# DeltaNet and Fourier mixing on one core: GpSimd's products and memsets on VectorE, transposed inverses as identity products, unread products ahead of the first load, inversions begun a slot sooner

## The chip, the core and the metric

The kernel runs on one core of a Trainium2 chip. A core has five engines, each with an instruction queue of its own that is worked off in order: TensorE (PE, matrix products into PSUM; PEld is its loading of weights), VectorE (DVE), ScalarE (ACT), GpSimd (POOL) and SyncE (SP, which issues transfers). They wait for one another by semaphores. The metric is the time of one execution on the device in microseconds (us); lower is better.

## The reference

Two blocks follow each other. The first is DeltaNet attention: for each of 4 batches and 8 heads, over 768 steps, with 48 numbers per head:

```python
k_n = k / (np.linalg.norm(k, axis=-1, keepdims=True) + 1e-06)
for t in range(S):
    y[:, :, t] = np.einsum('bhd,bhde->bhe', q[:, :, t], state)
    v_old = np.einsum('bhde,bhd->bhe', state, kt)
    state = state + bt[:, :, :, None] * np.einsum('bhd,bhe->bhde', kt, vt - v_old)
```

The second takes the output as x with 4 x 768 rows of 384 numbers, mixes it with a two-dimensional Fourier transform, and applies a layer norm and an MLP (384 to 1536 to 384):

```python
u = x + np.real(np.fft.fft(np.fft.fft(x, axis=1), axis=2))
un = (u - mean(u)) / np.sqrt(var(u) + 1e-06)
out = u + np.maximum(un @ w_ch1, 0.0) @ w_ch2
```

## The kernel before

**Attention in periods and rounds.** A period is 128 steps of all eight heads of one batch: 6 periods make a batch, 24 the whole (numbered g = 0 to 23). Inside a period the recurrence is turned into matrix products: with the Gram matrix of the keys (`pre_a`, in periods 0 to 11 by `gram16`, L351), the inverse of a triangular matrix, and products with it, so that only two steps per period (`step`, L671, c = 0 and 1) pass the state S on. The triangular systems of four periods are inverted together on VectorE; these four periods are a round (rounds 0 to 5). `invert16` (L451, rounds 0 to 2) inverts blocks of 16 and leaves the merging of two blocks to products on TensorE; `invert` (L392, rounds 3 to 5) inverts blocks of 32. Each starts with a memset of M (L467, L397) and a transpose of the Gram matrices (L468, L398), then runs a loop in which a product (L510, L439) and an addition (L513, L443) alternate, and ends with transposes: L516 writes the inverse into G, L518 the transposed inverse into A (L446 and L447 in `invert`).

`pre_m16` (L591) makes period g's matrix from its round's inverse. Z is the inverse with zeros in the other half of each pair (two ScalarE copies, L601). px, a product of the masked Gram matrix GU with Z, is copied as ND (L610); MT is the transposed inverse spread like Z (L614 on VectorE for period 0, otherwise L617 on ScalarE). Three groups of products with ND, MT and Z follow, and the values V are scaled by nT (L622). `pre_m` (L551) does less for periods 12 to 23: a masked copy MT (L559) and the scaled values (L562).

**The second block.** `folds` (L772) adds and subtracts halves of x for the Fourier step (L786, L788), `fourier` does its products, `mlp` (L889) the layer norm and the two matrix products, cut into pieces.

**The weights** arrive as 64-bit numbers and are converted on chip, in `weights` (L221): 12 pieces of w1 and 12 of w2, each by ScalarE copies (L272, L277), five VectorE operations (L278, L282, L283, L292, L294) and one product (L287).

**The order** of TensorE, VectorE, ScalarE and GpSimd is written out by hand, in program order; nothing reorders it. From L1082 on: keys 0 to 3, inversion 0, loads, keys 4 to 7, five products that nobody reads (`spin`, L1116), then batch 0's periods, with inversion 1 and the conversion of the weights in between (`fill`, `convert`). From batch 1 on, `period` (L991) runs six slots per period. In each slot come pieces of the two steps and of the next period's preparation, some operations of the running inversion (`advance(inv, ...)`), and pieces of the second block for the batch before, as many as `want` says. In periods that are the first or second of a round (li = 0 or 1) the keys of the next round are prepared; the inversion of the next round begins in slot 1 of li = 1.

PSUM tiles come from three tags with two buffers each: "pair" (two banks), "one" and "post". A tile that takes a buffer waits until the tile two before it under the same tag has been read. In `pre_m16` px is a "one" tile, while the products for S, for V's update, for the outputs and for turned keys with K are "pair" tiles.

Of the kernel before, what the change touches and what calls it, by code (L numbers as in the profile page):

```python
# [17 lines left out]
C = 64  # L18
L = 128
W = 32  # L20
RL = 4
# [43 lines left out]
def kernel(  # L65
# [37 lines left out]
    def ps_one():  # L103
        return ps.tile([128, 512], F32, tag="one", bufs=2, name="one")
# [87 lines left out]

    early = w2.rearrange("p c m -> p (c m)").rearrange("p (n h d) -> p n h d", h=8, d=64)
    nc.vector.memset(early[:, :, :, D:64], 0.0)
    early = [early[:, i] for i in range(9)]
# [25 lines left out]
    def weights():  # L221
# [13 lines left out]
        for last, pieces in enumerate(sets):  # L235
# [33 lines left out]
            for i in range(len(pieces) + 1):  # L269
# [10 lines left out]
                if i > 0:  # L280

                    nc.vector.tensor_scalar(num0, num0, 255, 2.0 ** 23, op0=ALU.min, op1=ALU.mult)  # L282
                    nc.vector.scalar_tensor_tensor(num0, hi0, -2 ** 31, num0, op0=ALU.bitwise_and,  # L283
                                                   op1=ALU.bitwise_or)
                    dst = pieces[i - 1][1]
                    c = dst.shape[1]
                    nc.gpsimd.tensor_tensor(dst, man0.rearrange("p (c f) -> p c f", c=c),  # L287
                                            num0.bitcast(F32).rearrange("p (c f) -> p c f", c=c),
                                            op=ALU.mult)
                    stage(i - 1 + deep)  # L290
# [60 lines left out]
    def gram16(g, KT, G):  # L351
# [5 lines left out]
        if first:  # L357
            GU = GXs["O"][:, g]
        else:
            GU = wk.tile([128, 8, C], F32, tag="GX", bufs=4, name="GU")  # L360
            nc.gpsimd.memset(GU[:, :, 0:V16], 0.0)
        GXs[g, 16] = GU
# [10 lines left out]
        for hh in range(2):  # L373
# [3 lines left out]
            else:  # L377
                nc.scalar.activation(dst[rw], src[rw, :, :, W:C], ACT.Copy)
        if g == 2 * RL - 1:
            yield  # L380
# [11 lines left out]
    def invert(r):  # L392
# [3 lines left out]
        M = wk.tile([128, W, W], F32, tag="M", name="M")  # L396
        nc.gpsimd.memset(M, 0.0)  # L397
        nc.vector.transpose(A, G.rearrange("p m s -> p s m"))  # L398
# [52 lines left out]
    def invert16(r):  # L451
# [14 lines left out]
        A, M, Ad, Md = whole(A2), whole(M2), blocks(A2), blocks(M2)  # L466
        nc.gpsimd.memset(M2, 0.0)  # L467
        nc.vector.transpose(A, G.rearrange("p m s -> p s m"))  # L468
# [47 lines left out]
        nc.vector.transpose(G.rearrange("p m s -> p s m"), M.rearrange("p t s -> p s t"))  # L516
        yield
        nc.vector.transpose(A.rearrange("p m t -> p t m"), M)  # L518
        rounds[r] = (A, G, nT)
        yield  # L520
# [30 lines left out]
    def pre_m(g):  # L551
# [9 lines left out]
                                op=ALU.mult)  # L561
        nc.gpsimd.tensor_tensor(V.rearrange("p c j d -> p (c j) d"),  # L562
                                V.rearrange("p c j d -> p (c j) d"),
# [27 lines left out]
    def pre_m16(g):  # L591
# [3 lines left out]
        K, GU = Ks[g % 3], GXs.pop((g, 16))  # L595
        MTd, Md, nT = rounds[r]
        m8 = slice(8 * li, 8 * li + 8)
        tags = ("QT", "LQ") if g < 2 * RL else ("WT", "WT")
        Z = wk.tile([128, 8, 2, W], F32, tag=tags[0], bufs=2, name="Z")
        for e in range(2):  # L600
            nc.scalar.activation(Z[:, :, e, :], Md[:, m8, :], ACT.Copy, scale=m_blk[:, e:e + 1])  # L601
        if g != 2 * RL:
            yield
        px = ps_one()
        for m in range(8):
            for hh in range(2):
                mm(px[full[hh], C * m:C * m + C], GU[full[hh], m, :],
                   Z[full[hh], m].rearrange("p b t -> p (b t)"), m == 0)
        ND2 = wk.tile([128, 8, C], F32, tag=tags[1], bufs=2, name="ND")
        nc.scalar.activation(ND2.rearrange("p m t -> p (m t)"), px, ACT.Copy)  # L610
        MT = wk.tile([128, 8, 2, W], F32, tag="MT", bufs=2, name="MT")
        for e in range(2):
            if g == 0:
                nc.vector.tensor_scalar(MT[:, :, e, :], MTd[:, m8, :], m_blk[:, e:e + 1], None,  # L614
                                        op0=ALU.mult)
            else:
                nc.scalar.activation(MT[:, :, e, :], MTd[:, m8, :], ACT.Copy,  # L617
                                     scale=m_blk[:, e:e + 1])

        def scaled_v():  # L620
            V = Vs.pop(g)
            (nc.vector if g < 2 * RL else nc.gpsimd).tensor_tensor(  # L622
                V.rearrange("p c j d -> p (c j) d"), V.rearrange("p c j d -> p (c j) d"),
                nT[:, m8, None].broadcast_to([128, 8, D]), op=ALU.mult)
            return V
# [146 lines left out]
    def folds(b):  # L772
# [11 lines left out]
        for t in range(TH):  # L784
            eng = nc.gpsimd if b and t < TH - 1 else nc.vector
            eng.tensor_tensor(E[:, 0, t], x[:, t], x[:, TH + t], op=ALU.add)  # L786
            yield
            eng.tensor_tensor(E[:, 1, t], x[:, t], x[:, TH + t], op=ALU.subtract)  # L788
            yield
# [198 lines left out]
    done = 0  # L988
    pm = inv = late = None

    def period(g, side):  # L991


        nonlocal pm, inv, late, done, fold
        b, n = divmod(g, NL)
# [33 lines left out]
        if not last_round and r > 1:  # L1029
            if li == 0:  # L1030
                load_beta(r + 1)
            keys = {0: ((0, 1), (2, 3), (4, 5)), 1: ((0, 1),)}.get(li, ())
            for i, (s0, s1) in enumerate(keys):
                k4 = pre_a(RL * (r + 1) + 3 * li + i)
                behind[s0].append(k4)
                pieces[s1].append(k4)
        for i in range(SLOTS):
# [5 lines left out]
            if i == 5 and n + 1 == NL:  # L1043
                o = outputs(g)
                drain(o)
                late = None
            if li == 1 and i == 1 and r > 1 and not last_round:
                inv = invert(r + 1)
# [11 lines left out]
            if b > 1:  # L1060
                want = 2 + (PIECES - KEEP - 2) * at // (SLOTS * NL)
            else:

                want = 2 + KF + (2 + 2 * KF) * at // (2 * SLOTS)
                if n > 1:
                    want = 4 + 3 * KF + (PIECES - KEEP - 4 - 3 * KF) * (at - 2 * SLOTS) // (
                        SLOTS * (NL - 2))
            for p in behind[i]:
# [7 lines left out]
    with tc.manual_schedule(engines=engines):  # L1076
# [4 lines left out]
        qs = [pre_q(g, QT6[:, g], LQ6[:, g]) for g in range(NL)]  # L1081
        ms = [pre_m16(g) for g in range(2 * RL)]  # L1082
        for g in range(RL):
            advance(keys[g])
            if g > 0:
                drain(keys[g - 1])
        drain(keys[RL - 1])
        advance(inv0, 2)
        for g in range(3):
# [21 lines left out]
        advance(keys[-1])  # L1111
        idle = wk.tile([128, DM], F32, tag="un", bufs=2, name="idle")
        nc.gpsimd.memset(idle, 0.0)
        unread = ps_post([128, 512], "unread")

        def spin(n):  # L1116

            for _ in range(n):
                nc.tensor.matmul(unread[:, 0:DM], lhsT=ident, rhs=idle, start=True, stop=True,  # L1119
                                 skip_group_check=True)  # L1120

        spin(5)

        advance(ms[0], 2)
        advance(qs[1])
# [10 lines left out]
        advance(inv1, 5)  # L1136
        drain(keys[-1])
        first = part(conv, 2 * KF + 2)
# [194 lines left out]
```

## Time and profile before

| | us |
|---|---|
| three runs, median (lowest, highest) | 760.11 (759.6, 760.41) |
| the profiled execution | 760.74 |
| its span, first to last instruction | 759.0 |
| busy in the span: ScalarE | 246.7 |
| busy in the span: GpSimd | 99.2 |
| GpSimd: 24 weight products L287 | 28.0 |
| GpSimd: 16 products of V (L562, L622) | 13.8 |
| GpSimd: 12 masked copies L559 | 12.8 |
| GpSimd: 12 folds (L786, L788) | 12.2 |
| GpSimd: memsets of M (L467, L397) | 6.0 |
| VectorE: 3 transposes L518 | 5.7 |

The profile is of one execution. Its view of groups gives, for each line, engine and shape of operand, the count, the sum and the mean time of one instruction, and what the engine waited for just before. The view by windows gives the busy time of each engine in a stretch of the span. The chain of waits is followed back from the last instruction: at each step to the instruction that released the one under view, or to the one before it on the same engine. Time on that chain is time that the span can lose; time elsewhere isn't, until the chain moves. Waits are the engine's idle time put down to the instruction that released it. For TensorE the largest of them:

```profile
PE pair L110 <- DVE S L732: 9.1, 6, 3.6
PE pair L110 <- DVE pair L745: 6.7, 3, 3.3
PE one L110 <- ACT Z L601: 6.3, 6, 2.5
PE pair L110 <- ACT QT L314: 5.6, 2, 4.6
```

The columns are the us in total, the number of waits and the longest one.

### The profile page before, as it was taken

What the parts mean: (1) busy time and instruction counts of PE and PEld (TensorE: products, weight loads), DVE (VectorE), ACT (ScalarE), POOL (GpSimd) and SP (SyncE); (2) the same over time, 40 slices, a digit from 0 to 9 for tenths busy, and PEclk for the clock granted to TensorE, in tenths of its full rate; (3) what the DMA queues carried; (4) which work ended last, traced back from release to release, by engine and by line L of the source; (5) the groups of instructions that cost most, each with busy time, mean ns of one, the idle gap of its engine ahead of it and who ended that gap; (6) DMA issues with size and microseconds to landing.
All of it is one profiled execution on the core that took longest, in us unless ns stands there. A gap on an engine that the chain in (4) does not pass through costs nothing.

```text
span 759.0 us, 23046 instructions
## 1 busy us (share of the span) xinstructions
PE 691.9 (91%) x10162; PEld 534.2 (70%) x10162; DVE 392.1 (52%) x961; ACT 246.7 (33%) x610; POOL 99.2 (13%) x138
## 2 busy tenths in 40 slices
PE   5877779697899986999999999999999999999998
PEld 4666668586667655877867768877667678777684
DVE  4966896879942499343298228178512240600000
ACT  3533662566424311223422333233223221211120
POOL 7000120322300012001110220020100110100000
PEclk9999987798999999999999999999999999999999
DMA  9832353025212312002212221011120000000000
GB/s 151 215 67 43 78 136 92 24 58 133 74 32 55 67 34 44 12 11 48 54 41 49 44 44 29 1 31 24 43 44 12 13 12 0 22 1 21 11 11 22
DMA packets 111863, 36.10 MB, mean 48 GB/s; under 512 B 101873, under 2 KB 109842, under 8 KB 111762
## 3 DMA queue, kind: packets, MB, share of 16 engines
q1 hardware_dynamic: 109938, 33.86, 20.3%
q8 instruction: 80, 1.31, 0.7%
q0 software_dynamic: 640, 0.43, 0.4%
q10 hardware_dynamic: 1184, 0.33, 0.3%
q14 instruction: 21, 0.17, 0.1%
HBM read 29.88 MB, written 4.72 MB: 46 GB/s over the span
## 4 chain that ended last, share of the span: by engine, by line
PE 74%; DVE 19%; ACT 3%; issue 3%; DMA 1%; DVEq 0%; ACTq 0%
PE po L110 24%; PE ph L110 21%; PE one L110 14%; PE pair L110 9%; PE one L113 2%; DVE M L443 2%; DVE tmp L439 2%; PE ptr L113 1%; DVE wtmp L294 1%; DVE wtmp L283 1%; PE unread L1119 1%; DMA C<-in_k_dram 1%; DVE M L513 1%; DVE wtmp L292 1%; PE pf L110 1%
## 5 line engine op out<-in xcount | busy, mean ns | idle before, releaser
L110 PE MATMUL ph<-unT,w 128*128 128x256 f32 x864 | 207.8, 392 | 0.7 <-ACT unT L911 0.7
L110 PE MATMUL po<-w,hT 128*128 128x384 f32 x576 | 204.7, 495 | 0.0
L110 PEld LDWEIGHTS ph<-unT,w 128*128 128x128 f32 x864 | 162.7, 194 | 25.5 <-issue 1.0
L110 PEld LDWEIGHTS po<-w,hT 128*128 128x128 f32 x576 | 103.5, 190 | 56.4
L921 ACT ACTIVATE hT<-ph 128x256 f32<-128x256 f32 x144 | 54.9, 382 | 148.5 <-PE ph L110 148.4
L932 DVE TENSOR_TENSOR x<-x,po 128x384 f32<-128x384 f32 x24 | 13.2, 550 | 107.0 <-PE po L110 107.0
L732 DVE TENSOR_TENSOR S<-S,pair 128x192 f32<-128x192 f32 x40 | 13.9, 348 | 73.4 <-PE pair L110 73.4
L110 PEld LDWEIGHTS one<-V,MT 64*64 64x64 f32 x768 | 29.5, 138 | 19.7 <-issue 8.9
L873 DVE TENSOR_TENSOR x<-x,one 128x193 f32<-128x193 f32 x24 | 8.5, 353 | 64.8 <-ACT Q L864 64.8
L110 PE MATMUL one<-V,MT 64*64 64x48 f32 x768 | 34.8, 225 | 3.8 <-DVE V L691 1.8
L443 DVE TENSOR_TENSOR M<-M,tmp 128x31 f32<-128x31 f32 (+15 forms) x93 | 35.1, 378 | 3.2
L439 DVE TENSOR_TENSOR tmp<-A,M 128x31 f32<-128x31 f32 (+15 forms) x93 | 33.5, 360 | 2.4
L110 PE MATMUL one<-MT,ND 64*64 64x64 f32 x768 | 29.1, 226 | 1.8 <-ACT MT L640 0.7
L691 DVE TENSOR_TENSOR V<-V,pair 128x192 f32<-128x192 f32 x33 | 11.5, 349 | 36.9 <-PE pair L110 33.2
L559 POOL TENSOR_TENSOR MT<-A,pack 128x512 f32<-128x512 f32 x12 | 12.8, 1065 | 131.1 <-PE one L110 64.4
L110 PEld LDWEIGHTS one<-dtab,F 97*128 97x128 f32 (+1 forms) x192 | 25.7, 193 | 5.3 <-ACT F L868 0.5
L110 PEld LDWEIGHTS one<-MT,ND 64*64 64x64 f32 x768 | 26.5, 141 | 2.9 <-issue 1.1
L314 ACT ACTIVATE QT<-one 128x512 f32<-128x512 f32 x24 | 14.3, 596 | 42.1 <-PE one L113 42.1
L287 POOL TENSOR_TENSOR w<-wtmp 128x384 f32<-128x384 f32 x12 | 14.6, 1217 | 89.7 <-DVE wtmp L283 89.7
L110 PE MATMUL pair<-KT 48*32 48x64 f32 (+1 forms) x1152 | 22.7, 247 | 4.0 <-ACT KT L314 3.9
L110 PEld LDWEIGHTS pair<-U,K 64*64 64x64 f32 x704 | 15.5, 135 | 15.3 <-issue 12.4
L110 PE MATMUL one<-dtab,F 97*128 97x97 f32 (+1 forms) x192 | 26.2, 277 | 0.0
(173 smaller groups left out, 1009.5 us busy)
## 6 DMA issues: line engine op xcount, KB each, us to landing
w<-in_moe_w_ch_dram SPq DMA_DIRECT2D x12, 384.0 KB
E<-in_moe_w_ch_dram SPq DMA_DIRECT2D x12, 384.0 KB
out_dram<-x SPq DMA_DIRECT2D x24, 192.0 KB
K<-in_k_dram SPq DMA_DIRECT2D x92, 48.0 KB
V<-in_v_dram SPq DMA_DIRECT2D x92, 48.0 KB
C<-in_k_dram SPq DMA_DIRECT2D x18, 192.0 KB
Q<-in_q_dram SPq DMA_DIRECT2D x18, 192.0 KB
w<-in_q_dram SPq DMA_DIRECT2D x6, 192.0 KB
```

The lines of the kernel that those rows point to most:

```text
L110: nc.tensor.matmul(o, lhsT=lhsT, rhs=rhs, start=start, stop=stop, skip_group_check=True)
L113: nc.tensor.matmul(o, lhsT=src, rhs=ident[0:src.shape[0], 0:src.shape[0]], is_transpose=True, start=start, stop=True, skip_group_check=True)
L287: nc.gpsimd.tensor_tensor(dst, man0.rearrange("p (c f) -> p c f", c=c), num0.bitcast(F32).rearrange("p (c f) -> p c f", c=c), op=ALU.mult)
L314: nc.scalar.activation(dst.rearrange("p h j t -> p (h j t)"), pt, ACT.Copy)
L439: nc.vector.tensor_tensor(t, A[:, j + 1:W, j:j + 1].broadcast_to([128, n, j + 1]), M[:, j:j + 1, 0:j + 1].broadcast_to([128, n, j + 1]), o ...
L443: nc.vector.tensor_tensor(M[:, j + 1:W, 0:j + 1], M[:, j + 1:W, 0:j + 1], t, op=ALU.add)
L559: nc.gpsimd.tensor_tensor(MT, MTd[:, m8, None, :].broadcast_to([128, 8, 2, W]), m_blk[:, None, :, None].broadcast_to([128, 8, 2, W]), op=A ...
L691: nc.vector.tensor_tensor(R4, R4, pw[:, :, 0:2 * D].rearrange("p a (j e) -> p a j e", e=D), op=ALU.subtract)
L732: nc.vector.tensor_tensor(s1v, s0.rearrange("p h j e -> p h (j e)"), pk, op=ALU.add)
L873: nc.vector.tensor_tensor(near, near, pb[:, 0, 0:MH + 1], op=ALU.add)
L921: nc.scalar.activation(hT[:, fc, :], ph, ACT.Relu)
L932: nc.vector.tensor_tensor(x[:, T, :], x[:, T, :], po, op=ALU.add)
```

## The change

- A tile `idle` of zeros is made first of all on VectorE, and four unread products run on TensorE ahead of the first transposes of keys; before the px of period 0 there are two instead of five, with `idle` as both operands instead of the identity matrix as weights.
- On VectorE instead of GpSimd: the 24 products that finish a weight piece, the memset of `idle`, the memset of GU in 8 periods, the memset of M in all rounds but the first, the product of V and nT in periods 8 to 23, and the folds of batches 1 to 3.
- Rounds 0 to 2: the transpose that made the transposed inverse (L518) is gone. `pre_m16` makes MT from products of Z with the identity matrix, 16 more products of 64x64 per period in 12 periods, in the second bank of px, which becomes a "pair" tile. MT is one copy instead of two. In period 0 the second half of Z and the copy of MT are on VectorE.
- At the start, the inversion's first transpose (L468) comes ahead of the masks of GU of keys 2 and 3, which come ahead of the inversion's further steps.
- In `period`, the last key of a round is prepared in slot 5 of li = 0 and slot 0 of li = 1 instead of slots 0 and 1 of li = 1, and the inversion begins in slot 0 of li = 1. Pieces of the second block in batch 1's six periods: up to 14, and then 13, 11, 4, 7, 7 and 6, instead of 14, then 13, 13 and four equal parts of 5.5; 62 in both cases.

```diff
@@ -191 @@
+    idle = wk.tile([128, DM], F32, tag="un", bufs=2, name="idle")
+    nc.vector.memset(idle, 0.0)
     nc.vector.memset(early[:, :, :, D:64], 0.0)
...
@@ -284 @@ weights
-                    nc.gpsimd.tensor_tensor(dst, man0.rearrange("p (c f) -> p c f", c=c),
+                    nc.vector.tensor_tensor(dst, man0.rearrange("p (c f) -> p c f", c=c),
...
@@ -358 @@ gram16
-            nc.gpsimd.memset(GU[:, :, 0:V16], 0.0)
+            nc.vector.memset(GU[:, :, 0:V16], 0.0)
...
-        if g == 2 * RL - 1:
+        if first or g == 2 * RL - 1:
             yield
...
@@ -394 @@ invert
-        nc.gpsimd.memset(M, 0.0)
+        nc.vector.memset(M, 0.0)
...
@@ -464 @@ invert16
-        nc.gpsimd.memset(M2, 0.0)
+        (nc.vector if r else nc.gpsimd).memset(M2, 0.0)
...
-        yield
-        nc.vector.transpose(A.rearrange("p m t -> p t m"), M)
-        rounds[r] = (A, G, nT)
+        rounds[r] = (None, G, nT)
...
@@ -559 @@ pre_m
-        nc.gpsimd.tensor_tensor(V.rearrange("p c j d -> p (c j) d"),
+        nc.vector.tensor_tensor(V.rearrange("p c j d -> p (c j) d"),
...
@@ -593 @@ pre_m16
         for e in range(2):
-            nc.scalar.activation(Z[:, :, e, :], Md[:, m8, :], ACT.Copy, scale=m_blk[:, e:e + 1])
+            if g == 0 and e:
+                nc.vector.tensor_scalar(Z[:, :, e, :], Md[:, m8, :], m_blk[:, e:e + 1], None,
+                                        op0=ALU.mult)
+            else:
+                nc.scalar.activation(Z[:, :, e, :], Md[:, m8, :], ACT.Copy,
+                                     scale=m_blk[:, e:e + 1])
         if g != 2 * RL:
             yield
-        px = ps_one()
+
+        px = ps_pair()
         for m in range(8):
             for hh in range(2):
-                mm(px[full[hh], C * m:C * m + C], GU[full[hh], m, :],
+                mm(px[full[hh], 0, C * m:C * m + C], GU[full[hh], m, :],
                    Z[full[hh], m].rearrange("p b t -> p (b t)"), m == 0)
+        for m in range(8):
+            for hh in range(2):
+                mm(px[full[hh], 1, C * m:C * m + C], Z[full[hh], m].rearrange("p b t -> p (b t)"),
+                   ident[full[hh], full[hh]], m == 0)
...
-        for e in range(2):
-            if g == 0:
-                nc.vector.tensor_scalar(MT[:, :, e, :], MTd[:, m8, :], m_blk[:, e:e + 1], None,
-                                        op0=ALU.mult)
-            else:
-                nc.scalar.activation(MT[:, :, e, :], MTd[:, m8, :], ACT.Copy,
-                                     scale=m_blk[:, e:e + 1])
+        if g == 0:
+            nc.vector.tensor_copy(MT.rearrange("p m b t -> p (m b t)"), px[:, 1])
+        else:
+            nc.scalar.activation(MT.rearrange("p m b t -> p (m b t)"), px[:, 1], ACT.Copy)
...
-            (nc.vector if g < 2 * RL else nc.gpsimd).tensor_tensor(
+            nc.vector.tensor_tensor(
...
@@ -782 @@ folds
-            eng = nc.gpsimd if b and t < TH - 1 else nc.vector
-            eng.tensor_tensor(E[:, 0, t], x[:, t], x[:, TH + t], op=ALU.add)
+            nc.vector.tensor_tensor(E[:, 0, t], x[:, t], x[:, TH + t], op=ALU.add)
...
@@ -1029 @@ period
-            keys = {0: ((0, 1), (2, 3), (4, 5)), 1: ((0, 1),)}.get(li, ())
...
+            if li == 0:
+                for i in range(3):
+                    k4 = pre_a(RL * (r + 1) + i)
+                    behind[2 * i].append(k4)
+                    pieces[2 * i + 1].append(k4)
+                last_key = pre_a(RL * (r + 1) + 3)
+                behind[5].append(last_key)
+            elif li == 1:
+                pieces[0].append(last_key)
...
-            if li == 1 and i == 1 and r > 1 and not last_round:
+            if li == 1 and i == 0 and r > 1 and not last_round:
                 inv = invert(r + 1)
...
-                want = 2 + KF + (2 + 2 * KF) * at // (2 * SLOTS)
-                if n > 1:
-                    want = 4 + 3 * KF + (PIECES - KEEP - 4 - 3 * KF) * (at - 2 * SLOTS) // (
-                        SLOTS * (NL - 2))
+                want = 2 + KF
+                for of in (13, 11, 4, 7, 7, 6):
+                    want += of * min(max(at, 0), SLOTS) // SLOTS
+                    at -= SLOTS
...
@@ -1080 @@
+        spin(4)
         for g in range(RL):
             advance(keys[g])
             if g > 0:
-                drain(keys[g - 1])
+                advance(keys[g - 1])
+            if g > 1:
+                drain(keys[g - 2])
+        advance(keys[RL - 1])
+        advance(inv0)
+        drain(keys[RL - 2])
         drain(keys[RL - 1])
-        advance(inv0, 2)
+        advance(inv0)
...
@@ -1109 @@
-        spin(5)
-
-        advance(ms[0], 2)
+        spin(2)
+
+        advance(ms[0])
+        drain(keys[-1])
+        advance(ms[0])
```

## The prediction

> **What bounds the kernel now.** I read the engine totals and the 40 slices first, then sums of busy time by stage, then the chain of waits inside each stage where TensorE was short of work, then the groups of VectorE and GpSimd by form, because a fixed price hides in none of the first three.
>
> From the page:
> ```profile
> PE 691.9 (91%) x10162; PEld 534.2 (70%) x10162; DVE 392.1 (52%) x961; ACT 246.7 (33%) x610; POOL 99.2 (13%) x138
> ...
> PE   5877779697899986999999999999999999999998
> ...
> DVE  4966896879942499343298228178512240600000
> ```
> TensorE is the bound from slice 16 on (303 us) and GpSimd is nearly idle. The sums by stage, cut at the places where the chain changes its nature (columns: length, then busy us of PE, PEld, DVE, ACT, POOL, then granted clock, DMA share, GB/s):
> ```profile
> 0.00:37.00 37.00, 26.59 (x370) 19.59 (x370) 25.75 (x63) 16.38 (x40) 16.11 (x42) 1.00 1.05 186
> 37.00:79.00 42.00, 30.40 (x1049) 28.24 (x1049) 28.20 (x73) 17.98 (x40) 0.00 (x0) 0.96 0.28 53
> 79.00:118.00 39.00, 28.74 (x1036) 26.02 (x1028) 34.22 (x73) 22.38 (x49) 9.09 (x8) 0.90 0.43 109
> 162.00:213.00 51.00, 42.71 (x507) 34.00 (x506) 49.12 (x124) 25.10 (x62) 14.31 (x16) 0.90 0.34 89
> 256.00:303.00 47.00, 36.87 (x737) 26.55 (x737) 43.63 (x105) 9.90 (x25) 6.91 (x7) 1.00 0.18 39
> 303.00:759.00 456.00, 446.96 (x5140) 335.62 (x5136) 167.78 (x430) 119.17 (x310) 38.96 (x50) 1.00 0.11 25
> ```
> VectorE is full in 162-213 and 256-303. TensorE idles 58 us before 303 and 9 us after. So whatever a part does after 303 is worth little unless it is TensorE work, and before 303 a part is worth what the chain there says. Three pieces of the chain of waits (start, length, what):
> ```profile
> 29.54 6.04 PE unread L1119 x10
> 35.58 1.10 PE one L110 x32
> ...
> 256.41 0.28 ACT G L346
> 256.69 0.02 issue
> 256.72 1.96 DVE A L398
> ...
> 300.73 1.85 DVE G L447
> 302.58 0.21 DVE S L732
> ```
> The first: five unread products keep TensorE until 35.58, though the Z that px needs was written by 34.31 (timeline). The second: the inversion of round 3 starts when the last key's G is copied (256.72) and holds VectorE to 302.58. Last the forms of three rows:
> ```profile
> L294 DVE TENSOR_SCALAR wtmp<-w 128x384 int32<-128x384 int32 x12 | 11.1, 926 | 0.4
> ...
> L622 DVE TENSOR_TENSOR V<-V,nT 128x384 f32<-128x384 f32 x8 | 4.4, 546 | 0.0
> ```
> ```profile
> L287 POOL TENSOR_TENSOR w<-wtmp 128x384 f32<-128x384 f32 x12 | 14.6, 1217 | 89.7 <-DVE wtmp L283 89.7
> ```
> The same product costs GpSimd 1.22 us and VectorE about 0.55. And the VectorE conversion L294, which runs beside it, takes 926 ns where the same operation on the other tile takes 473 as a mean and 347 in its undisturbed instances. Summed over all VectorE instructions that overlap a GpSimd one, the excess over undisturbed ones of the same form is about 25 us.
>
> **What the Trainium skill says.** "SBUF — State Buffer", section "Who interferes with whom": VectorE and GpSimd share one port pair as an exclusive lock, contended by VectorE operations with two SBUF inputs or in a 2-port mode. The 926 against 347 ns agrees. "GPSIMD Engine Reference", 4.1: two-input elementwise work is about twice as slow on GpSimd; 1217 against 546 ns agrees. "TensorE: Matmul & The Clock Gate", Part 1: the array runs at half clock until about 3.4 us of sustained activity, and drops back after an idle window. The trace agrees: 128x128 transposes start every 225 ns before 34.8 us, every 128 ns later, and an unread record takes 0.61 us against 0.34 for one of the same width later. The page's digit 9 in the first slices has no clock record behind it. Further clock records at half speed lie at 41.6-45.0, 109.9-123.5, 137.2-147.4, 174.7-181.5, 195.2-198.6 and 304.4-307.8 us.
>
> **The change part by part.** The profiled execution (span 759.0, 760.74 with what lies around it) is what the sum is made against; the median, 760.11, is 0.63 below it.
>
> *VectorE.* It gains 24 w products, 8 GU memsets, 5 of the M memsets, one idle memset, 16 V products and 12 folds; at 0.5, 0.08-0.2, 1.0, 1.0, 0.55 and 0.55 us that is about 12 + 1.2 + 5 + 1 + 8.7 + 6.6 = 34.5 us. It loses three transposes L518 (5.7) and most of the 25 us of stretching; the mask product L559 (1.07 us, 12 times) and rstd stay on GpSimd and keep perhaps 4 of it. Net +4 to +8 us of VectorE time, of which only what falls in full stretches counts.
>
> *TensorE.* Twelve groups of 16 identity products (64x64): a group like them takes 1.10-1.16 us in the chain, 0.95 when nothing hinders it, 1.8 at half clock; 11-14 us in all, eight groups before 160 us, four in 213-303. The copy of MT follows the second group instead of the first, but is one copy of 0.60 us instead of two of 0.50. px moves from the two "one" buffers to the two "pair" buffers that the S, K and LQ products of the loop use as well, so a px waits for the reader of the pair two before it, and the next state product waits for both ND and MT copies; queued behind it are all of TensorE's next groups. The trace of before doesn't show that wait: between 0 (TensorE idle there anyway) and 1.2 us (the copies ND and MT in sequence) per turn; I take 0.4.
>
> *0-37 us.* Four unread products ahead of load 0, cold at 1.22 us each, run from about 1.5 to 6.4 us (they wait for a memset of 1.0) and hold the first transposes from 4.81 to 6.4, those of load 1 from 6.62 to 7.5. If the clock is up by then, the six groups of 1.05 us between 6.62 and 13.03 halve, limited by the loads that land every 1.3 us, and the transpose L468 starts at about 13.1 instead of 16.65. Two masks (2 x 0.69) and three GU memsets (0.6) then stand between it and the inversion's next step on VectorE, with its square root on ScalarE (ends 18.75 now) hidden under them: that step from 18.78 to about 17. L516 ends 1.9 earlier; Z's halves are made on two engines at once (0.5 instead of 0.9); two unread products instead of five no longer outlast Z; px and the identity group take 2.2, the MT copy 0.7: first product at about 35.2 against 37.35, -2.2. If the clock is not up, 0.9 is lost at the start and the end is about +0.8. I take -1.5.
>
> *37-79.* Four turns, each +1.0 for the identity group where TensorE is on the chain, +0.15 for the copies, +0.4 for the buffers, less what falls into the stage's 11.6 us of idle (28%): about 4 x 0.75 = +3; L518 leaves the chain at 75.48 (0.94): together +2 (0 to +5).
>
> *79-118.* VectorE's chain: seven L294 lose 0.69 of stretch, seven products cost 0.5, a memset 0.2: -1.1; four turns of identity and buffer waits at +0.5: together +0.9 (-1 to +4).
>
> *118-162.* TensorE runs half-clocked for much of it. Nothing here ties the clock to the change for certain: 0, from -5 (the clock holds) to +2. Conversions: stretch gone about as much as products added, 0.
>
> *162-213.* VectorE is the bound (49.1 of 51): +6.0 for 12 products, +1.0 memset, +0.6 GU memsets, +0.5 V, against 8.3 us of stretch here: -0.2 (-3 to +3).
>
> *213-303.* The last key and the inversion start one slot sooner, and the early slots give fewer MLP pieces: priced by rows, TensorE's work between px of period 8 (213.36) and the last key's gram falls from 37.8 to 34.0, its two identity groups included; scaled to the traced 43.0, -4.3 us. The moved step takes along one load of 192 KB on SP's queue (DMA share 0.18-0.30 here, free) and on VectorE the memset M (1.0, VectorE is idle before 256). The inversion keeps its length: stretch gone 3.2, V products +1.1, folds +2.2. TensorE has 10.1 us idle in 256-303; 4.3 earlier with two further identity groups of 1.1 leaves 3-4, so TensorE allows it: -4. The 3.56 us wait at 302.83 shrinks with it, and the half clock of 304.4-307.8 with that, -1.5. Together -5.5 (-8 to -1).
>
> *303 to the end.* Bound by TensorE with 9 us idle. Inversions a slot sooner save at most the gaps at 522.75 (1.50) and 538.65 (0.82). V products now stand in VectorE's order ahead of the S updates and wait for their loads, which land 0.6 to 2.2 us after the S updates now start; the products reading S have 1.0 to 3.1 us to spare, so at most +0.5. -0.8 (-2 to +2).
>
> Sum: -1.5 + 2 + 0.9 + 0 - 0.2 - 5.5 - 0.8 = -5.1: 755.6 against the profiled 760.74, 755.0 against the median.
>
> **The rivals.** *TensorE and its pair buffers become the bound before 160 us* (the slower end): each of the eight early turns pays the whole identity group and the wait for both copies. For it: 70% TensorE share there is an average over short alternations, each of which is on the chain. Against it: the idle of 28%. At +1.8 per turn the stages to 118 give +0.8, +6 and +6 instead of -1.5, +2, +0.9; with the rest as above +6.3, 766.4 profiled, 765.8. It decides from about 1.3 us per turn, where the gain of 213-303 is used up.
>
> *The clock holds*: the added early TensorE work keeps the activity up, and the half clock at 41.6 and 109.9-123.5 goes: -2.2, +1, +0.5, -5, and the rest: about -12.5, 747.6. For it: each half-clock record follows a stretch of waits. Against: the waits of 79-118 are VectorE's and stay.
>
> *The inversion's head start is given back*: it starts 4.3 us sooner, but folds and V products lengthen it or another engine holds the S behind it; -1 instead of -5.5: 759.5. For it: 43.6 us of VectorE in 47. That the change doesn't do what it says is excluded by the instruction lists, except that the clock may not be up at load 0, which is in the bounds.
>
> **How the numbers follow.** The forecast has 0.45, with its own range 751 to 759; the slower rival 0.29; the clock 0.13; the given-back start 0.13. A difference under 0.2% (1.5 us) can't be told from none. Faster: 0.45 x 0.97 + 0.13 + 0.13 x 0.3 = 0.61; same: 0.08; slower: 0.31. The range takes in half of the rivals on either side: 747 to 766.
>
> **What would show it.** Right: the first product of period 0 at 35 us and L468 at 13; L294 near 350 ns in both forms; the round-3 transpose L398 at or before 253 with no wait over 1 us at its end; clock records near 1.0 from 7 us. Wrong: TensorE waits of about 1 us on ND or MT copies in every turn before 118 us; the conversions' stage longer than 51 us; L398 starting no sooner than about 4 us ahead of where it would, counted from px of period 8.

## The result

The changed kernel takes 770.11 us (median of 4 runs, 768.71 to 771.2) against 760.25 for the kernel before beside it: 1.013 times, 95% interval 1.0112 to 1.0149. It is slower by 9.9 us where 5.1 us less were forecast, and above the range. The profiled execution of it took 769.61 us, with a span of 767.8.

From the page of the changed kernel:

```profile
PE 700.4 (91%) x10548; PEld 543.7 (71%) x10548; DVE 395.7 (52%) x1024; ACT 243.4 (32%) x598; POOL 39.1 (5%) x72
...
PE   6677786798799898999999999999999999999998
...
PEclk8599998899899999999999999999999999999999
```

GpSimd lost 60 us of work and VectorE gained 3.6, just under the 4 to 8 of the sum; TensorE gained 8.5, where 11 to 14 were counted. What is new stands in the first slices: TensorE is less busy there and its clock lower.

The sums by stage, cut where the same places of the program lie now (columns as before):

```profile
0.00:41.00 41.00, 27.99 (x404) 20.52 (x404) 23.27 (x66) 17.20 (x43) 14.13 (x36) 0.71 1.02 176
41.00:83.00 42.00, 30.29 (x1064) 28.05 (x1064) 27.14 (x72) 13.37 (x28) 0.00 (x0) 1.00 0.24 43
83.00:123.00 40.00, 30.57 (x1100) 28.42 (x1100) 31.02 (x74) 21.11 (x44) 0.00 (x0) 0.96 0.40 97
172.00:223.00 51.00, 42.85 (x511) 34.37 (x509) 46.35 (x139) 26.66 (x65) 1.04 (x2) 0.90 0.34 93
265.00:312.00 47.00, 43.54 (x834) 31.49 (x834) 40.80 (x108) 10.46 (x24) 1.04 (x1) 1.00 0.20 42
312.00:768.00 456.00, 445.51 (x5140) 335.42 (x5140) 177.11 (x453) 118.78 (x310) 19.89 (x29) 1.00 0.11 25
```

How far the changed kernel is behind at the same instruction, from its start in both traces:

| place | before, us | after, us | behind, us |
|---|---|---|---|
| first product with MT of period 0 | 37.35 | 41.60 | 4.25 |
| first update of S in batch 0 | 47.95 | 52.12 | 4.2 |
| last update of S in batch 0 | 117.71 | 128.24 | 10.5 |
| px of period 8 | 213.36 | 223.25 | 9.9 |
| start of round 3's inversion (L398, now L400) | 256.72 | 262.16 | 5.4 |
| its last transpose (L447, now L449) | 300.73 | 309.25 | 8.5 |
| last update of S in the trace | 612.52 | 621.39 | 8.9 |

So 4 us are lost before 42 us and 6 more in batch 0. From its end to px of period 8 the lag hardly changes (10.5 to 9.9), and up to the end of round 3's inversion 1.4 us are given back.

**The start.** The timeline of the kernel before (start, length, engine, line, operation, tiles; in brackets, where there is any, the idle time before and who ended it):

```profile
7.64 1.13 PE L110 MATMUL pair<-KT 48*64 48x64 f32 x32
...
16.57 1.89 DVE L468 STREAM_TRANSPOSE A<-G 128x1024 f32<-128x1024 f32 x1
...
35.50 1.15 PE L110 MATMUL one<-Z,GU 64*64 64x64 f32 x32
```

And of the changed kernel:

```profile
10.92 0.69 DVE L385 TENSOR_TENSOR GU<-pair,pack 128x512 f32<-128x512 f32 x1
11.75 0.69 PE L110 MATMUL pair<-KT 48*64 48x64 f32 x32 [1.63 <-DVE GU L385]
13.79 0.69 DVE L385 TENSOR_TENSOR GU<-pair,pack 128x512 f32<-128x512 f32 x1
14.63 1.13 PE L110 MATMUL pair<-KT 48*64 48x64 f32 x32 [2.19 <-DVE GU L385]
17.13 1.91 DVE L470 STREAM_TRANSPOSE A<-G 128x1024 f32<-128x1024 f32 x1
...
36.63 1.85 PE L110 MATMUL pair<-Z,GU 64*64 64x64 f32 x32 [3.62 <-ACT GU L390]
38.27 1.93 PE L110 MATMUL pair<-pack,Z 64*64 64x64 f32 x32
40.23 0.60 ACT L620 ACTIVATE ND<-pair 128x512 f32<-128x512 f32 x1 [3.65 <-PE pair L110]
40.86 0.69 DVE L623 COPY MT<-pair 128x512 f32<-128x512 f32 x1 [5.33 <-ACT ND L620]
41.60 1.15 PE L110 MATMUL one<-MT,ND 64*64 64x64 f32 x32 [0.80 <-DVE MT L623]
```

The early unread products do what they are for: the Gram groups up to 11.75 take 0.69 us where a Gram group took 1.13. But the mask L385 of a key reads the pair tile of its Gram product, and it now stands in VectorE's queue behind the copies of the next key (L378). The diff above moves the masks of keys 0 and 1 too; the description of the change names only those of keys 2 and 3. There are two pair buffers. So the third Gram product waits 1.63 us for the first key's mask and the fourth 2.19 for the second's. The fourth takes 1.13 us again, because the clock has fallen. The view by windows, cut where the granted clock changes, has 1.00 and then 0.50 in its third column from the end:

```profile
6.10:12.90 6.80, 4.47 (x114) 3.40 (x112) 2.39 (x5) 3.43 (x7) 6.40 (x12) 1.00 1.43 157
12.90:33.40 20.50, 14.56 (x216) 10.63 (x216) 17.22 (x56) 10.14 (x28) 2.16 (x4) 0.50 1.08 204
```

Full clock lasts from 6.1 to 12.9 us, then half clock to 33.4. The two waits are not shown to be what ends it: the traces of the experiments in which they are short lose the full clock at about the same time (see the first experiment). At the end of the start px, now a pair tile, waits for key 7's mask on ScalarE, which stands behind Z; TensorE has by then been idle for 3.6 us, and px and the identity group run at half clock, 1.85 and 1.93 us.

**The turns of batch 0.** One turn before, and the same one after:

```profile
88.66 1.09 PE L110 MATMUL one<-Z,GU 64*64 64x64 f32 x30 [0.58 <-ACT Z L601]
89.85 0.60 ACT L610 ACTIVATE ND<-one 128x512 f32<-128x512 f32 x1 [0.87 <-PE one L110]
...
90.68 0.45 PE L110 MATMUL pair<-S,WT 48*64 48x48 f32 x16 [0.43 <-DVE S L732]
```

```profile
98.34 1.15 PE L110 MATMUL pair<-Z,GU 64*64 64x64 f32 x32 [0.97 <-ACT x L762]
...
99.32 1.03 PE L110 MATMUL pair<-pack,Z 64*64 64x64 f32 x29
...
100.46 0.60 ACT L620 ACTIVATE ND<-pair 128x512 f32<-128x512 f32 x1 [2.18 <-PE pair L110]
100.96 0.59 ACT L625 ACTIVATE MT<-pair 128x512 f32<-128x512 f32 x1
...
101.60 0.45 PE L110 MATMUL pair<-S,WT 48*64 48x48 f32 x16 [0.73 <-ACT MT L625]
```

From the start of px to the product of S and WT it took 2.02 us and takes 3.26 in this turn. The step's products are queued behind the identity group, and then wait for the pair that px holds until MT is copied (0.73 us). Over the stage from the first to the last update of S:

```profile
48.00:118.00 70.00, 50.95 (x1856) 46.67 (x1852) 54.82 (x126) 34.85 (x75) 9.09 (x8) 0.94 0.34 78
```

```profile
52.50:128.50 76.00, 55.43 (x2005) 51.35 (x2000) 52.52 (x132) 32.77 (x68) 0.00 (x0) 0.96 0.31 73
```

TensorE's busy time rose by 4.5 us and the stage by 6.0: its idle time, 19.0 us before, is 20.6 after. The added work did not fill it.

**VectorE's forms.** The stretching is gone as the prediction said (changed kernel, groups by form):

```profile
L289 DVE TENSOR_TENSOR w<-wtmp 128x384 f32<-128x384 f32 x12 | 6.7, 558 | 0.4
...
L296 DVE TENSOR_SCALAR wtmp<-w 128x384 int32<-128x384 int32 x12 | 4.3, 356 | 0.4
```

The last weight operation (L294 before, L296 now) takes 356 ns instead of 926, and the product beside it 558 instead of 1217.

### The profile page after: what moved, and what is told of

It is laid out like the page before. It is cut to its first block, busy times and chain, and to the rows that moved or that the text cites. A ratio compares the mean times of both kernels' runs of the same rounds, so it can differ in the third digit from the quotient of the medians.

```text
span 767.8 us, 23680 instructions
## 1 busy us (share of the span) xinstructions
PE 700.4 (91%) x10548; PEld 543.7 (71%) x10548; DVE 395.7 (52%) x1024; ACT 243.4 (32%) x598; POOL 39.1 (5%) x72
## 4 chain that ended last, share of the span: by engine, by line
PE 74%; DVE 17%; ACT 5%; issue 2%; DMA 1%; SPq 0%; DVEq 0%; ACTq 0%
PE po L110 23%; PE ph L110 21%; PE one L110 13%; PE pair L110 12%; PE one L113 2%; DVE M L445 2%; DVE tmp L441 2%; PE ptr L113 1%; DVE M L515 1%; DVE tmp L512 1%; DMA E<-in_moe_w_ch_dram 1%; DVE G L518 1%; ACT Z L605 1%; DVE w L289 1%; DVE A L400 1%
## 5 line engine op out<-in xcount | busy, mean ns | idle before, releaser
L445 DVE TENSOR_TENSOR M<-M,tmp 128x31 f32<-128x31 f32 (+15 forms) x93 | 33.5, 360 | 3.2
L698 DVE TENSOR_TENSOR V<-V,pair 128x192 f32<-128x192 f32 x33 | 11.6, 352 | 43.1 <-PE pair L110 43.0
L441 DVE TENSOR_TENSOR tmp<-A,M 128x31 f32<-128x31 f32 (+15 forms) x93 | 31.7, 340 | 2.2
L110 PE MATMUL pair<-KT 48*32 48x64 f32 (+1 forms) x1152 | 21.1, 237 | 7.8 <-DVE GU L385 3.8
L110 PE MATMUL pair<-Z,GU 64*64 64x64 f32 x384 | 15.0, 234 | 13.9 <-ACT Z L605 5.0
L110 PEld LDWEIGHTS pair<-KT 48*32 48x32 f32 (+1 forms) x1152 | 17.3, 127 | 11.8 <-ACT KT L316 6.0
```

What stands on the lines that cost most here:

```text
L110: nc.tensor.matmul(o, lhsT=lhsT, rhs=rhs, start=start, stop=stop, skip_group_check=True)
L441: nc.vector.tensor_tensor(t, A[:, j + 1:W, j:j + 1].broadcast_to([128, n, j + 1]), M[:, j:j + 1, 0:j + 1].broadcast_to([128, n, j + 1]), o ...
L445: nc.vector.tensor_tensor(M[:, j + 1:W, 0:j + 1], M[:, j + 1:W, 0:j + 1], t, op=ALU.add)
L698: nc.vector.tensor_tensor(R4, R4, pw[:, :, 0:2 * D].rearrange("p a (j e) -> p a j e", e=D), op=ALU.subtract)
```

## The experiments

Each number is a ratio of medians to the kernel before measured beside it, with its 95% interval. One execution of the kernel before differs from the next by more here than in the first measurement: 759.1 to 765.3 us beside the first four experiments.

**Four parts, each undone alone in the changed kernel.** First the key order at the start:

```diff
-        if first or g == 2 * RL - 1:
+        if g == 2 * RL - 1:
             yield
...
             if g > 0:
-                advance(keys[g - 1])
-            if g > 1:
-                drain(keys[g - 2])
-        advance(keys[RL - 1])
-        advance(inv0)
-        drain(keys[RL - 2])
+                drain(keys[g - 1])
         drain(keys[RL - 1])
-        advance(inv0)
+        advance(inv0, 2)
```

> The changed kernel with one part undone: the masks of keys 0 to 3 come again right behind their own Gram copies, ahead of the next key's, and L468's transpose after them all. Theory A (the new order makes the Gram products of keys 2 and 3 wait for a pair buffer, 1.6 and 2.2 us at 11.75 and 14.63 us, and the idle costs the clock that the early unread products gained): those two waits go, the first transpose starts near 13 instead of 17.1, the first product of period 0 near 38 to 39 instead of 41.6, and the time falls by 2 to 4 us to about 767. Rival B (identity products and pair buffers in the loop): the start moves, but what follows absorbs it or is set by other waits; 769 to 770. Rival C (VectorE's load): no difference, 770.

Measured: 1.0067 (1.0039 to 1.0094). A second measurement of the changed kernel itself gave the yardstick:

> The changed kernel once more, as the yardstick beside the others of this call: 1.013 times the kernel before, give or take 0.3%.

Measured: 1.012 (1.0101 to 1.014). So the key order is worth about 0.5%, 4 us, and theory A holds for that part of the loss, not for the rest. In its trace the Gram products of keys 2 and 3 wait 0.42 and 0.90 us instead of 1.63 and 2.19, the transpose L470 starts at 14.69 and the first product with MT at 37.81 instead of 41.60. What theory A says of the clock is not borne out: full clock ends at 12.1 us here, and in the six later runs that have the early unread products and these short waits at 11.8 to 16.5, against 11.2 to 13.8 in the six traces with the long waits. The traced execution happens to be the slowest of the eight (771.99 us against a median of 767.73), and in it the gain of the start is gone by the end of batch 0; the 4 us rest on the medians.

Second, the identity products: L518 put back, px again a "one" tile, MT two copies from the transposed inverse, both halves of Z in period 0 on ScalarE again, and key 7's mask back in its old place. The main lines of the edit:

```diff
-        px = ps_pair()
+        px = ps_one()
...
-                mm(px[full[hh], 1, C * m:C * m + C], Z[full[hh], m].rearrange("p b t -> p (b t)"),
-                   ident[full[hh], full[hh]], m == 0)
...
+        nc.vector.transpose(A.rearrange("p m t -> p t m"), M)
+        rounds[r] = (A, G, nT)
```

> The changed kernel with the identity products undone: the transposed inverse is again made by a VectorE transpose, px is again a one-bank tile with its own two buffers, MT two ScalarE copies (VectorE for period 0). Theory A (prologue order): the first product still comes late, near 39, and the time falls by 2 us or less, to 768 or above. Rival B (identity products and the pair buffers cost about 1 us in each of the eight early turns): the time falls by 5 to 8 us, to 762 to 765, and the waits of TensorE on ND or MT copies ahead of products with S go. Rival C: three more VectorE transposes, so slower by 1 to 2 us.

Measured: 0.999 (0.9971 to 1.0009), 1.3% or 9.9 us less than the changed kernel; rival B, and more than it expected. Rival C falls; what the three VectorE transposes cost by themselves is not told apart here.

Third, GpSimd gets its work back:

> The changed kernel with the weight products, memsets (but that of idle), products of V and folds back on GpSimd. Theories A and B, in which the work on VectorE is neutral: 769 to 772. Rival C (VectorE's load lengthens 79-118, 162-213 and the inversions of rounds 3 to 5): 764 to 767. If sharing of the port is what binds there, slower, 773 to 776, with the last weight operation at 926 ns on one of its tiles again.

Measured: 1.0138 (1.0099 to 1.0177). That is the yardstick's 1.012 within the interval: theory C falls.

Fourth, the slot of the inversion, the last key and the pieces of batch 1 (the main line of the edit):

```diff
-            if li == 1 and i == 0 and r > 1 and not last_round:
+            if li == 1 and i == 1 and r > 1 and not last_round:
                 inv = invert(r + 1)
```

> The changed kernel with the last key, the start of the inversion and the pieces of batch 1 as before. If the head start of the inversion gains what the trace suggests (the lag behind the kernel before falls from 9.9 us at px of period 8 to 7.9 after the inversion), slower by 2 to 3 us: 772 to 773. If the whole of the 5.5 us of the prediction is gained and given back by other parts, slower by 5: 775. If the head start is worth nothing: 770.

Measured: 1.0163 (1.0124 to 1.0202), 0.4% or 3 us slower than the changed kernel, though the two intervals just overlap (1.012 had 1.0101 to 1.014). If it is a gain, it has the size read from the lag, not the size predicted; e9 below shows the gain by itself.

**Whether the two losses add.** Key order and identity products undone together:

> The changed kernel with two parts undone together: the old key order at the start and the VectorE transposes in place of the identity products. If the two costs (about 0.6% and 1.4% when each was undone alone) are separate and add, 0.993 times the kernel before, some 755 to 758 us, and the first product of period 0 no later than in the kernel before. If both act through the same thing (the clock at the start and the late first period), little is added to the second alone: 0.999.

Measured: 0.9945 (0.9929 to 0.996), a median of 757.9. The two losses are separate: 0.5% and 1.3% undone alone, 1.75% together. What is left of the change is faster than both kernels. The first product with MT stands at 35.94 us in its trace, 1.4 earlier than in the kernel before.

**What in the identity products costs.** First the buffers (the main lines; the later periods keep the pair tile):

```diff
-        px = ps_pair()
+        if g < NL:
+            px0, px1 = ps_one(), ps_post([128, 512], "px1")
```

> The changed kernel, but in periods 0 to 5 px takes a one-bank tile of its former kind and the identity products one of the tag post, which is idle then; so the products stay and the pair buffers are not taken. Theory B1 (the waits for pair buffers are what the identity products cost): the time falls by 6 to 9 us, to 1.002 to 1.005 times the kernel before. Theory B2 (the products themselves, on TensorE's chain and at half clock in the first group, and the single copy behind them): it falls by 0 to 3 us, 1.009 to 1.013.

Measured: 1.0112 (1.0085 to 1.0139). The waits of S and WT on MT copies are gone from its trace, and in a turn at 97 us px and the product of S and WT are 2.31 us apart instead of 3.26. But the time is that of the changed kernel: by the two intervals the difference lies between 3 us less and 2 us more, so the 6 to 9 us of theory B1 are excluded. In the profiled execution more half clock stands in batch 0 (0.91 against 0.96), so a small gain may be hidden. Then the products alone, back in e5's kernel, in a bank that nothing reads:

```diff
+        if g < NL:
+            px1 = ps_post([128, 512], "px1")
+            for m in range(8):
+                for hh in range(2):
+                    mm(px1[full[hh], C * m:C * m + C], Z[full[hh], m].rearrange("p b t -> p (b t)"),
+                       ident[full[hh], full[hh]], m == 0)
```

> The kernel of e5 (old key order, VectorE transposes) with the identity products of periods 0 to 5 put back in their place behind px, into a bank that nobody reads. Theory B2a (their TensorE time of about 1 us each, 1.9 in period 0, is on the chain though TensorE is idle for 28% there): 6 to 8 us slower than e5, 1.002 to 1.005 times the kernel before, and a step with S lags about 1 us more per period up to 118 us. Theory B2b (the cost is the copy of MT behind the products, or px held by pair buffers): as e5, 0.9945, or at most 2 us more.

Measured: 1.0014 (0.9993 to 1.0034), 0.7% or 5.3 us slower than e5 (by the two intervals 3 to 7), though nothing waits for the result. Shared among the six groups that is 0.9 us each, a little below the expectation of B2a. Its stage of batch 0 and that of e5:

```profile
47.50:120.90 73.40, 55.89 (x1986) 52.00 (x1981) 54.20 (x134) 34.89 (x75) 0.00 (x0) 0.93 0.33 75
```

```profile
47.20:117.80 70.60, 52.36 (x1858) 48.05 (x1853) 54.29 (x134) 35.06 (x75) 0.00 (x0) 0.94 0.35 78
```

3.5 us more of TensorE, 2.8 us more of the stage: again the idle time was hardly used. The traces don't show the even growth that B2a expected, though. The lag behind e5 is 2.7 us at the second update of S (54.26 against 51.51), 3.1 at the end of batch 0, and only after 204 us, where the unread products are long done, does it rise from 2.9 to 5.1. A comparison over all traces is steadier. From the first product with MT to the last update of S in batch 0 the nine traces without identity products have 79.1 to 83.4 us (median 80.8), the seven with all of them 84.9 to 90.2 (88.3), and e8 84.2. So the products themselves bring about half of what the whole construction costs there. The other half is not in e8, where nothing reads their result. In e6, which has no pair tile there and took 88.4, it remains, so the copy of MT behind the second group is left as the likely cause; it was not tried by itself, nor were the six later groups.

**Which part of the key order.** Masks 0 and 1 back behind their copies, the transpose still ahead of masks 2 and 3:

```diff
-            if g > 1:
-                drain(keys[g - 2])
+            if g in (1, 2):
+                drain(keys[g - 1])
```

> The changed kernel, but the masks of keys 0 and 1 come again right behind their own copies; the inversion's transpose stays ahead of the masks of keys 2 and 3. If the waits of the Gram products of keys 2 and 3 for a pair buffer are the cost (theory A): as e1 or a little better, 1.005 to 1.007 times the kernel before, and no wait of a Gram product on a mask before 15 us. If the masks and memsets ahead of the inversion's next step are the cost: 1.011 to 1.013.

Measured: 1.0085 (1.0058 to 1.0112), between the two expectations; the interval still touches that of the changed kernel. Its timeline:

```profile
10.49 0.69 PE L110 MATMUL pair<-KT 48*64 48x64 f32 x32 [0.41 <-DVE GU L385]
...
12.08 0.69 PE L110 MATMUL pair<-KT 48*64 48x64 f32 x32 [0.90 <-DVE GU L385]
14.15 1.91 DVE L470 STREAM_TRANSPOSE A<-G 128x1024 f32<-128x1024 f32 x1
```

The waits of 1.63 and 2.19 us are down to 0.41 and 0.90, L470 starts 3.0 us sooner and the first product with MT 3.1 us sooner (38.53 in place of 41.60), of the 3.8 that the whole key order brings in e1. In these traces the place of masks 0 and 1 is thus most of what the key order costs at the start. With the transposes back as well:

> The kernel of e12 with the VectorE transposes in place of the identity products: what is left of the change is the early unread products, the transpose ahead of masks 2 and 3, GpSimd's work on VectorE and the slot. If the transpose's place gains: 0.992 to 0.994 times the kernel before; if not, as e5, 0.9945 to 0.996.

Measured: 0.9972 (0.9951 to 0.9993), no better than e5. The transpose's new place gains nothing that can be told.

**The gains, each alone.** The slot and GpSimd's work together, with the start of the kernel before (in this run and the next two the five unread products have `idle` as both operands, as in the changed kernel; what that alone does was not tried):

> The kernel before with only GpSimd's work on VectorE and the inversions begun a slot sooner: key order, transposes and unread products (five, none ahead of load 0) as before. Theory (these two parts gain together what the lag shows between period 8 and the end of the inversion, 3 to 5 us): 0.993 to 0.996 times the kernel before. If the early unread products gain in e5, this is slower than e5 by 1 to 2 us; if they are worth nothing, the same.

Measured: 0.9961 (0.9939 to 0.9983). Then each of them:

> The kernel before with only the last key, the inversion's start and batch 1's pieces changed; GpSimd keeps its work. If this part and the moved work gain only together (undone alone in the changed kernel, each took the whole gain after 213 us away): 0.999 to 1.001 times the kernel before. If the head start is worth its 4 us by itself: 0.994 to 0.996.

Measured: 0.9959 (0.9939 to 0.9979).

> The kernel before with only GpSimd's products and memsets on VectorE. If the two parts gain only together: 0.999 to 1.002, with the inversion of round 3 no shorter and started no sooner. If the freed port is what gained in e7: 0.996.

Measured: 0.9975 (0.996 to 0.9989). The expectation that they gain only together was wrong: each gains alone, and the two together no more than the slot. e5 without GpSimd's part says the same within its interval:

> The kernel of e5 with GpSimd's work left on GpSimd: what is left of the change is the early unread products and the slot. If the moved work adds nothing once the slot is moved: as e5 and e9, 0.9945 to 0.996. If it gains 0.25% as it did alone: 0.997.

Measured: 0.9968 (0.9951 to 0.9986), against e5's 0.9945 (0.9929 to 0.996): a gain of 0.2% of the moved work there is possible, and not settled. What belongs to the slot, the place of the last key, the start of the inversion and the pieces of batch 1, was not taken apart.

The inversion of round 3 in the chain of waits of e9 (slot alone):

```profile
249.86 1.97 DVE A L400
...
297.48 1.82 DVE G L449
```

and of e10 (GpSimd's work alone):

```profile
257.44 1.98 DVE A L400
...
300.19 1.86 DVE G L449
```

From its first transpose to the end of its last it took 45.9 us in the kernel before, takes 49.4 in e9 and 44.6 in e10. Begun 6.9 us sooner than before in e9, it ends 3.3 sooner. That goes with the slot in every trace: 47.9 to 50.4 us in the fourteen traces with the new slot, 44.6 to 45.9 in the three with the old one.

**The unread products.** Three instead of two ahead of px, on e5's kernel:

> The kernel of e5 with three unread products ahead of px of period 0 instead of two, so that TensorE is busy up to the moment when Z is written, as in the kernel before. If the half clock of px and the next group in e5 (1.97 and 1.62 us instead of 1.15) comes from the idle time after the second unread product, the first product of period 0 comes 0.8 to 1.5 us sooner than in e5 and the time is 0.992 to 0.994 times the kernel before; if the clock's window sets it, as e5, 0.9945.

Measured: 0.996 (0.9943 to 0.9978). In the profiled execution the first update of S in batch 0 came 2.2 us sooner than in e5's, and at the update of S near 202 us the kernel was 2.2 us behind it: the gain didn't last. Between these two places the granted clock was 0.85 on average in e11's trace and 0.89 in e5's. Early products and two ahead of px, or none and five (e5 against e7): 0.9945 against 0.9961, the intervals overlap.

## Why the prediction was wrong

- *0-37 us* was put at -1.5 and is +4.25. The step that failed is "the six groups of 1.05 us between 6.62 and 13.03 halve ... and the transpose L468 starts at about 13.1". The groups halve as far as 12.9 us, but the transpose (now L470) starts at 17.13: the masks of keys 0 and 1, moved behind the next key's copies, hold the two pair buffers. The sum counts the masks of keys 2 and 3, as VectorE time behind the transpose; that those of keys 0 and 1 move too, and which buffer they release, isn't in it. With them back in place (e12) the transpose starts at 14.15. The bound "if the clock is not up ... about +0.8" was too narrow for the same reason: the clock was up at load 0, and the time was lost all the same.
- The same part priced px and the identity group at "2.2" at full clock; at half clock they took 3.6, and px waited for key 7's mask, which the pair buffer brought ahead of it.
- *37-79* and *79-118* were put at +2 and +0.9 and are +6.3 together. The step that failed is "less what falls into the stage's 11.6 us of idle (28%)". From the first to the last update of S TensorE has 4.5 us more work, and its idle time is 20.6 us where it was 19.0. The group is queued in front of the step's own products, as the turn shows, so it delays their results, and idle times that are waits for those results move along with it. e8 shows that the products alone cost 3 to 7 us for six groups. e6 shows no cost of the pair buffers; its interval leaves at most 3 us for six turns, so the 0.4 us per turn is not excluded. The rival "each of the eight early turns pays the whole identity group and the wait for both copies" had the mechanism: up to 118 us it comes to 12.8, against 10.5 measured. Its total of 765.8 is 4 us too low mainly because it keeps the whole gain of 213-303. Whether its second half, the wait for both copies, is real was not tried by itself; the traces speak for it.
- *118-213*: -0.2 and measured -0.6 (10.5 to 9.9). That fits an even exchange of GpSimd's stretching for its work on VectorE, as worked out, within what single traces can tell.
- *213-303* was put at -5.5; the lag fell from 9.9 to 8.5 at the inversion's end. Right was the start, 4.5 us sooner against px of period 8 (9.9 to 5.4; -4.3 was worked out). Wrong was "The inversion keeps its length": it grew from 45.9 to 49.0 us. The inversion's operations stand in VectorE's order between the updates of S and V and the sums of `pre_m16` (L645, L649), and begun earlier it meets these before TensorE has made their products. During the inversion VectorE waits for TensorE in the changed kernel

```profile
DVE S L739 <- PE pair L110: 2.4, 1, 2.4
DVE MT L649 <- PE one L110: 1.2, 1, 1.2
```

and, with a third wait of 0.3, for 3.9 us in all; in the kernel before that view has no wait for TensorE during the inversion. In e9 such waits make 2.9 us and the inversion is 3.6 us longer than in the kernel before, without any moved work, so the V products and folds aren't needed for it. This is the rival "The inversion's head start is given back", in about the size it named.
- *303 to the end*: -0.8 and measured +0.4 (8.5 to 8.9).

In the traces 14 us lie between the sum, -5.1, and the measured +8.9: 5.75 in the start, 3.4 in batch 0, 4.1 in 213-303 and 1.2 after it, less 0.4 in 118-213. What the change gains, the slot and GpSimd's work, is real (0.4% in e7) and about a quarter of the 1.75% that the two losses make together.

## What to carry to other kernels

TensorE idled for 27% of batch 0, and yet instructions added to its queue were not paid out of that idle time, because the products behind them were on the chain: ask what is queued behind an added instruction, not how busy the stage is. When a read of a PSUM tile is moved, count the tiles of its tag that are asked for in between: here the move held a buffer, and TensorE waited up to 2.19 us for it. And a chain on one engine that is interleaved with work waiting for another may gain only part of a head start: here 3.3 of 6.9 us.

## What the runs showed of the hardware

Executions of one kernel differ with the clock that TensorE was granted: beside the first four experiments the kernel before took 759.1 to 760.3 us in the six fastest runs, all at a mean clock of 0.975, and 764.7 to 765.3 in the six slowest, at 0.961 to 0.966. Half-clock stretches in the traces are 3.4 us long or multiples of it (6.8, 10.2, 20.5), but for the last one of a trace, which its end cuts off. The same part of the program meets them in one execution and not in another: of the two traces of the changed kernel one has such a stretch at 70.4 us and none at 84.6, the other the reverse. A gain of 2 us at the start was gone 150 us later in e11, with a lower clock in between; that the clock is the whole reason is not shown. Differences of some 2 us between single traces are thus not to be relied on, and the conclusions rest on the ratios of medians where there are any.

In period 0 the copy of MT on VectorE began only when ScalarE's copy of ND from the other bank of the same tile had ended (40.86, released at 40.83), though its own products had ended at 40.20. Whether the program's semaphores or the hardware ask for that was not tried.
